# Running part of a layer norm under the attention of the layer before it

## The chip, the cores and the metric

The kernel runs on one core of one Trainium2 chip. The metric is the time of one execution on the device in microseconds (us), median of several runs; lower is better. Engines are named as in the profile: PE (TensorE matmuls), PEld (its weight loads), ACT (ScalarE), DVE (VectorE), POOL (GpSimd), SP (which issues DMAs). Each takes instructions from a queue of its own, in order, and waits on semaphores for the others.

## The reference

Four attention layers, alternately of kind A (segmented causal attention with a compressive memory) and B (full attention), work on x of shape 2048 x 512, each on a layer norm of x and added to x. There are 32 heads of 16 features.

```python
x = A_x
x = x + _A_ref(_layernorm(x), A_wq, A_wk, A_wv, A_wo, A_beta)   # layer 0
x = x + _B_ref(_layernorm(x), B_wqkv, B_wo)                     # layer 1
x = x + _A_ref(_layernorm(x), A_wq, A_wk, A_wv, A_wo, A_beta)   # layer 2
x = x + _B_ref(_layernorm(x), B_wqkv, B_wo)                     # layer 3
```

## The kernel before

The 2048 tokens are 16 tiles of 128. A layer has these stages: norm with transposes of all 16 tiles; projections; (A only) the memory; attention; output projection with residual. A small scheduler gathers operations in program order, tracks who reads and writes which buffer or PSUM bank, and puts in the semaphore waits. Each engine's queue has the order in which the operations were added. So the place of an `add` call in the program decides what stands behind what.

```python
def ln_stage1(self, t):                       # statistics, then the root on ACT
    sc.add("dve", ... e.bn_stats(st[:, 0:6], xt) ...)
    sc.add("dve", ... e.bn_aggr(st[:, 6:8], st[:, 0:6]) ...)
    sc.add("act", ... e.activation(st[:, 8:9], st[:, 7:8], ACT.Sqrt, bias=eps) ...)

def ln_stage2(self, t, evac_eng="act"):       # normalise, transpose, evict
    sc.add("dve", ... e.reciprocal(st[:, 9:10], st[:, 8:9]) ...)
    sc.add("dve", ... e.tensor_scalar(xn, xt, mean, rstd, op0=subtract, op1=mult) ...)
    bank = self.misc_bank()
    for c in range(NCH):                      # 4 transposes of 128x128 into one PSUM bank
        sc.add("pe", ... e.transpose(...) ...)
    sc.add("act", ... e.activation(xT tile t, bank, ACT.Copy) ...)

def ln_all(self, evac_eng="act"):
    LA = 2
    for t in range(min(LA, NT)):
        self.ln_stage1(t)
    for t in range(NT):
        if t + LA < NT:
            self.ln_stage1(t + LA)
        self.ln_stage2(t, evac_eng=evac_eng)
# [cut]
def layer_B(self, li):
    self.ln_all(...)
    ...                                       # K, Q and V projections; some are deferred
    self._misc_banks = [6, 7]
    for qc in range(4):                       # chunk of 512 queries
        for h in range(H):                    # a "pair": one head, one chunk
            for g in range(6):
                self.b_unit(...)              # 2 or 3 score matmuls (PE), one exp (ACT)
                if prev is not None and 1 <= g <= 4:
                    self.b_pv_part(*prev, g - 1, pstate)   # P.V of the pair before (PE)
                    ...                       # g == 4: its normalisation on DVE
                if g == 5 and work:
                    work.pop(0)()             # one outproj_T, outproj_mm or projection
    ...
    work.extend(outproj_items(3))             # the last four tiles: the "tail"
    self._misc_banks = list(range(8))
    while work:
        work.pop(0)()
# outproj_T(t):  4 transposes (PE), copy of the bank to xT (DVE)
# outproj_mm(t): 4 matmuls of 512 columns (PE), residual addition into x (DVE)
```

After the tail of one layer the next layer's norm starts. Six PSUM banks feed the exponentials, in two groups of three; the other two (6 and 7) take turns for P.V and all work that is slipped in at a pair's end.

The softmax here doesn't subtract the row's maximum and nothing guards it: scores larger than these inputs give would overflow.

## Time and profile before

| | |
|---|---|
| median of the first 4 runs | 2698.26 us (2697.51 to 2699.76) |
| span of the profiled run, mean granted PE clock | 2696.3 us, 0.965 |
| ACT, PE, DVE busy | 87%, 80%, 29% |
| last exponential of layer 1 to first projection matmul of layer 2 | 36.3 us |
| of this: last P.V and output projection of four tiles, then norm of layer 2 | 15 us, 21.5 us |

Times in a timeline are the start and the length of a group of equal instructions; the bracket gives the idle time of the engine before it and what ended that. First the page: busy times, and the costliest group (line, engine, operation, output and input, count; then busy us and mean ns; then idle us before and what ended most of it).

```profile
PE 2166.5 (80%) x26976; PEld 1242.6 (46%) x26976; DVE 778.4 (29%) x2571; ACT 2344.4 (87%) x2098; POOL 13.5 (1%) x19
...
L794 ACT ACTIVATE pT<-ps 128x1536 bf16<-128x1536 f32 (+1 forms) x1536 | 1877.9, 1317 | 112.8 <-PE ps L786 90.9
```

The exponentials of the two B layers (L794) are most of the time. The timeline of ACT at the start of layer 1's second chunk of queries shows how full ACT is. Six exponentials are one pair.

```profile
617.63 14.78 ACT L794 ACTIVATE pT<-ps 128x1536 bf16<-128x1536 f32 x12
632.90 14.78 ACT L794 ACTIVATE pT<-ps 128x1536 bf16<-128x1536 f32 x12 [0.48 <-PE ps L786]
648.16 14.78 ACT L794 ACTIVATE pT<-ps 128x1536 bf16<-128x1536 f32 x12 [0.49 <-PE ps L786]
663.43 14.78 ACT L794 ACTIVATE pT<-ps 128x1536 bf16<-128x1536 f32 x12 [0.49 <-PE ps L786]
```

In these pairs the output projection of the chunk before is slipped in, alternately four transposes and four matmuls. ACT has a gap only every second pair: after the matmuls. So PE can take four transposes per pair for nothing, and four 512-column matmuls cost ACT 0.49 us.

The timeline at the end of layer 1 (lines chosen) shows the stretch that the change is about. Its first line holds the last exponentials, which end at 1336.63.

```profile
1329.29 7.34 ACT L794 ACTIVATE pT<-ps 128x1536 bf16<-128x1536 f32 x6
...
1338.72 0.61 PE L843 MATMUL ps<-ident,tok 128*128 128x128 bf16 x4 [0.54 <-DVE tok L831]
1339.37 0.42 DVE L853 COPY xT<-ps 128x512 bf16<-128x512 bf16 x1 [0.70 <-PE ps L843]
1339.85 1.89 PE L864 MATMUL ps<-woB,xT 128*128 128x512 bf16 x4 [0.52 <-DVE xT L853]
1341.78 0.69 DVE L868 TENSOR_TENSOR x_tok<-x_tok,ps 128x512 bf16<-128x512 bf16 x1 [1.98 <-PE ps L864]
...
1344.78 0.69 DVE L868 TENSOR_TENSOR x_tok<-x_tok,ps 128x512 bf16<-128x512 bf16 x1 [1.98 <-PE ps L864]
...
1356.93 0.69 DVE L444 BATCH_NORM_STATS2 lnst<-x_tok 128x6 f32<-128x512 bf16 x1
1357.65 0.18 DVE L445 BATCH_NORM_AGGREGATE lnst<-lnst 128x2 f32<-128x6 f32 x1
1357.75 0.13 DVE L457 RECIPROCAL lnst<-lnst 128x1 f32<-128x1 f32 x1
1357.92 0.41 DVE L458 TENSOR_SCALAR xn_ring<-x_tok,lnst 128x512 bf16<-128x512 bf16 x1
1358.25 0.69 DVE L444 BATCH_NORM_STATS2 lnst<-x_tok 128x6 f32<-128x512 bf16 x1
...
1372.97 1.49 PE L495 MATMUL ps<-xT,wproj 128*128 128x512 bf16 x3
```

A tile's output projection takes 3.0 us (1341.78 to 1344.78). Its four matmuls take 1.89 us, 0.43 us each from issue to issue, against 0.22 us in mid-attention (there two score matmuls take 0.59 us and three 0.81 us). The clock granted to PE is 0.50 here (windows view, 1338 to 1350 us); the recorded texts call PE at this rate cold. The Trainium skill (TensorE: Matmul & The Clock Gate, "What's actually happening") describes a PE clock that halves after an idle window and rises again after a busy one; the factor of two agrees with this trace. In the norm, DVE has no idle time: 1.31 us a tile (1356.93 to 1358.25). ACT does the root and the eviction beside it, and has nothing else to do there.

### The profile page before, as it was taken

The page shows a single profiled execution, that of the slowest core. Times are in us where ns is not written, and L with a number is a line of the kernel's source. Part 1 is how long each engine was busy: PE and PEld are TensorE (multiplying, and loading weights), DVE is VectorE, ACT ScalarE, POOL GpSimd, SP SyncE. Part 2 cuts the span into 40 slices and gives each one's busy share as a digit, 9 for nine tenths or more (in the row PEclk, how much of TensorE's full clock was granted, in tenths as well). Part 3 has the DMA queues.
Part 4 walks back from the last instruction along what each step waited for, and adds up shares of the span by engine and source line. Part 5 has one row for each costly group of instructions (what it writes and reads, how often), then busy time and mean ns, then how long its engine had stood idle before and what let it go on. Part 6 is the DMA issues. An engine that isn't in the chain of part 4 may idle for free.

```text
span 2696.3 us, 62861 instructions
## 1 busy us (share of the span) xinstructions
PE 2166.5 (80%) x26976; PEld 1242.6 (46%) x26976; DVE 778.4 (29%) x2571; ACT 2344.4 (87%) x2098; POOL 13.5 (1%) x19
## 2 busy tenths in 40 slices
PE   6788788888888888888776887888888888888887
PEld 2465444444444444444434664444444444444444
DVE  6777732111111111111177776321111111111111
ACT  6488658999999999999863886689999999999997
POOL 1000000000000000000000000000000000000000
PEclk9799899999999999999977997999999999999998
DMA  2000000000000000000000000000000000000000
GB/s 71 24 2 2 1 1 2 25 2 2 1 2 2 1 2 2 2 2 2 1 1 24 2 2 2 1 1 2 2 1 9 2 2 9 2 1 2 9 2 9
DMA packets 9919, 15.56 MB, mean 6 GB/s; under 512 B 432, under 2 KB 8624, under 8 KB 9648
## 3 DMA queue, kind: packets, MB, share of 16 engines
q1 hardware_dynamic: 9648, 11.54, 1.3%
q8 instruction: 219, 3.59, 0.6%
q14 instruction: 52, 0.43, 0.1%
HBM read 9.45 MB, written 2.10 MB: 4 GB/s over the span
## 4 chain that ended last, share of the span: by engine, by line
ACT 51%; PE 30%; issue 14%; DVE 5%; DMA 0%; ACTq 0%; SPq 0%
ACT pT L794 45%; PE ps L786 11%; ACT pT L729 5%; PE ps L495 4%; PE ps L715 3%; PE ps L864 3%; PE ps L510 2%; PE ps L749 2%; PE ps L720 1%; PE ps L813 1%; PE ps L465 1%; DVE xn_ring L458 1%; DVE amem L664 1%; DVE lnst L444 1%; PE ps L843 1%
## 5 line engine op out<-in xcount | busy, mean ns | idle before, releaser
L794 ACT ACTIVATE pT<-ps 128x1536 bf16<-128x1536 f32 (+1 forms) x1536 | 1877.9, 1317 | 112.8 <-PE ps L786 90.9
L786 PE MATMUL ps<-qm,kT 128*128 128x512 bf16 x4096 | 1122.2, 377 | 369.5 <-ACT pT L794 274.2
L813 PEld LDWEIGHTS ps<-v_aug,pT 128*128 128x128 bf16 x16384 | 558.7, 96 | 244.5 <-ACT pT L794 1.7
L786 PEld LDWEIGHTS ps<-qm,kT 128*128 128x128 bf16 x4096 | 301.9, 96 | 769.8 <-PE ps L813 343.2
L813 PE MATMUL ps<-v_aug,pT 128*128 128x17 bf16 x16384 | 563.0, 171 | 1.5 <-ACT pT L794 1.5
L827 DVE RECIPROCAL small<-ps 128x4 f32<-128x4 f32 x256 | 46.9, 183 | 1499.7 <-PE ps L813 1499.7
L729 ACT ACTIVATE pT<-ps 128x1280 bf16<-128x1280 f32 x256 | 308.1, 1236 | 123.4 <-PE ps L720 119.5
L715 PE MATMUL ps<-qm,kT 128*128 128x512 bf16 (+3 forms) x1024 | 225.2, 301 | 5.4 <-DVE qm L686 4.8
L686 DVE TENSOR_SCALAR qm<-qT,blockmask_f 128x512 bf16<-128x512 bf16 x512 | 177.9, 349 | 88.4 <-PE ps L786 88.4
L720 PE MATMUL ps<-negmask,ident 128*128 128x128 bf16 x1024 | 184.1, 220 | 0.0
L749 PE MATMUL ps<-v_aug,pT 128*128 128x17 bf16 x2560 | 104.9, 172 | 38.9 <-ACT pT L729 36.3
L495 PE MATMUL ps<-xT,wproj 128*128 128x512 bf16 x512 | 126.4, 402 | 0.0
L715 PEld LDWEIGHTS ps<-qm,kT 128*128 128x128 bf16 x1024 | 99.8, 97 | 57.4 <-DVE qm L686 5.4
L749 PEld LDWEIGHTS ps<-v_aug,pT 128*128 128x128 bf16 x2560 | 82.3, 96 | 84.2 <-ACT pT L729 82.9
L720 PEld LDWEIGHTS ps<-negmask,ident 128*128 128x128 bf16 x1024 | 100.2, 98 | 2.8
L465 PE MATMUL ps<-ident,xn_ring 128*128 128x128 bf16 x256 | 38.2, 307 | 64.0 <-DVE xn_ring L458 64.0
L510 PE MATMUL ps<-wproj,xT 128*128 128x512 bf16 x384 | 84.7, 379 | 0.2 <-DVE phqT L543 0.2
L495 PEld LDWEIGHTS ps<-xT,wproj 128*128 128x128 bf16 x512 | 52.8, 103 | 66.9 <-issue 13.0
L768 DVE SCALAR_TENSOR_TENSOR tok<-tmpo,gcol,amem 128x64 bf16<-128x64 f32 x256 | 73.0, 285 | 9.1
L757 DVE RECIPROCAL small<-ps 128x4 f32<-128x4 f32 x256 | 46.8, 183 | 81.6 <-PE ps L749 71.6
L472 ACT ACTIVATE xT<-ps 128x512 bf16<-128x512 bf16 x64 | 37.6, 597 | 31.6 <-PE ps L465 31.6
L868 DVE TENSOR_TENSOR x_tok<-x_tok,ps 128x512 bf16<-128x512 bf16 x64 | 43.9, 685 | 63.5 <-PE ps L864 63.5
(60 smaller groups left out, 845.1 us busy)
## 6 DMA issues: line engine op xcount, KB each, us to landing
wproj<-in_B_wqkv_dram SPq DMA_DIRECT2D x2, 1536.0 KB, 6.4
x_tok<-in_A_x_dram SPq DMA_DIRECT2D x4, 512.0 KB, 5.4
out_dram<-x_tok SPq DMA_DIRECT2D x4, 512.0 KB, 2.9
wproj<-in_A_wq_dram SPq DMA_DIRECT2D x2, 512.0 KB, 5.8
wproj<-in_A_wk_dram SPq DMA_DIRECT2D x2, 512.0 KB, 6.9
wproj<-in_A_wv_dram SPq DMA_DIRECT2D x2, 512.0 KB, 7.5
woA<-in_A_wo_dram SPq DMA_DIRECT2D x1, 512.0 KB, 9.1
woB<-in_B_wo_dram SPq DMA_DIRECT2D x1, 512.0 KB, 9.2
```

Of the source, the lines that this page charges most:

```text
L495: sc.add("pe", (lambda lhsT, rhs, cin: lambda e: e.matmul(self.ps[:, bank.col0:bank.col0 + 512], lhsT, rhs, start=(cin == 0), stop=(cin == ...
L510: sc.add("pe", (lambda lhsT, rhs, cin: lambda e: e.matmul(self.ps[:, bank.col0:bank.col0 + 512], lhsT, rhs, start=(cin == 0), stop=(cin == ...
L686: sc.add("dve", lambda e: e.tensor_scalar(dst, src, mcol, None, op0=ALU.mult), reads=[self.b_qT[c][n + i] for i in range(4)] + [self.b_blo ...
L715: sc.add("pe", (lambda out_ap, lhsT, rhs: lambda e: e.matmul(out_ap, lhsT, rhs, start=True, stop=False))(out_ap, lhsT, rhs), reads=[kreads ...
L720: sc.add("pe", (lambda mask_out: lambda e: e.matmul(mask_out, self.ident[:], self.negmask[:], start=False, stop=True))(mask_out), reads=[s ...
L729: sc.add("act", lambda e: e.activation(dst, src, ACT.Exp, scale=float(SCALE)), writes=gr, bank_ops=[(B0, "r", alloc), (B1, "r", alloc), (B ...
L749: sc.add("pe", (lambda out_ap, lhsT, rhs, kb, qb: lambda e: e.matmul(out_ap, lhsT, rhs, start=(kb == 0), stop=(kb == qb)))(out_ap, lhsT, r ...
L768: sc.add("dve", lambda e: e.scalar_tensor_tensor(dst, tmpo, omg, am, op0=ALU.mult, op1=ALU.add), reads=[b_tmpo, self.b_gcol] + [self.b_ame ...
L786: sc.add("pe", (lambda out_ap, lhsT: lambda e: e.matmul(out_ap, lhsT, qmap, start=True, stop=True))(out_ap, lhsT), reads=[self.b_kT[c][kt] ...
L794: sc.add("act", lambda e: e.activation(dst, src, ACT.Exp, scale=float(SCALE)), writes=gr, bank_ops=[(banks[i], "r", alloc) for i in range( ...
L813: sc.add("pe", (lambda out_ap, lhsT, rhs, kt: lambda e: e.matmul(out_ap, lhsT, rhs, start=(kt == 0), stop=(kt == 15)))(out_ap, lhsT, rhs, kt),
L864: sc.add("pe", (lambda lhsT, rhs, c: lambda e: e.matmul(self.ps[:, bank2.col0:bank2.col0 + 512], lhsT, rhs, start=(c == 0), stop=(c == NCH ...
```

## The change

The layers become generators that yield after each step, and a driver lets the next layer advance by one step per pair of the present layer. A `need`/`done` table holds back what isn't ready. It does so only where the next layer is an A, so only between layers 1 and 2, and only for the norm: layer 2's projections still need the end of layer 1. Tiles 0 to 11 of x are final during layer 1 (after its chunks 0 to 2), tiles 12 to 15 only in its tail. So that ACT isn't burdened under the attention, the fused norm takes its root as a power of -0.5 on POOL and evicts on DVE. Core of the diff:

```diff
+    def ln_stage1(self, t, on_pool=False):
         ... bn_stats, bn_aggr ...
-        sc.add("act", ... ACT.Sqrt ...)
+        if not on_pool:
+            sc.add("act", ... ACT.Sqrt ...)
+            return
+        sc.add("dve", lambda e: e.tensor_scalar(st[:, 8:9], st[:, 7:8], float(LN_EPS), None, op0=ALU.add), ...)
+        sc.add("pool", lambda e: e.tensor_tensor(st[:, 9:10], st[:, 8:9], self.mhalf[:, 0:1], ALU.pow), ...)
 # [cut: ln_stage2 split into ln_stage2 (normalise) and ln_T (transpose, evict)]
+    def gen_A(self, li, fused_head):
+        for t in range(NT):
+            while s1 < NT and s1 <= t + LA:
+                if s1 > t and ("x", prev, s1) not in self.done:
+                    break
+                yield ("need", ("x", prev, s1))
+                self.ln_stage1(s1, on_pool=fused_head)
+                s1 += 1
+            self.ln_stage2(t, on_pool=fused_head)
+            if fused_head:
+                yield ("step", "norm")
+                if ("x", prev, 12) not in self.done:
+                    yield ("step", "norm")
+            self.ln_T(t, evac_eng=("dve" if fused_head else "act"))
+            yield ("step", "ln")
+        bank_fn = self.all_bank_rr()
+        yield ("need", ("end", prev))          # projections wait for the end of the layer before
 # [cut: the rest of gen_A and gen_B follows layer_A and layer_B, with ("done", ...) marks]
+    def drive(self):
+            fused = (li > 0) and self.fuse and kind == "A"
+        while cur < len(gens):
+            r = advance(cur)
+            ...
+            if self.fuse and nl < len(gens) and self.layers[nl] == "A" and cur in in_attn and nl not in in_attn:
+                for _ in range(self.fuse_steps):
+                    r2 = advance(nl)
```

## The prediction

> **What bounds the kernel.** The page gives ACT 87% busy of 2696.3 us, PE 80%, and a chain that ended last of which 45% is the B layers' exponentials. The timeline of ACT in the first B layer shows them back to back: 7.44 us per head-and-chunk pair. It also shows what extra PE work at a pair's end costs: four transposes alone, no ACT gap; four output-projection matmuls, a gap of 0.49 us; two projection groups, 1.35 us. So about 0.4 us of PE work per pair is free (4 x 0.215 us of matmul minus 0.49); the rest is lost.
>
> **What the change does.** Only a layer A that follows a layer B is fused, so of four layer norms one (layer 2's) moves: tiles 0 to 11 go under layer 1's attention, tiles 12 to 15 into its output-projection tail. The projections stay behind the end of layer 1. The reciprocal root moves from ACT (square root, 0.29 us, and table loads of 1.28 us) to a power on POOL; the eviction from ACT (0.60 us) to DVE (0.42 us by the outproj copies of the same shape).
>
> **What is on the path.** In the timeline around layer 1's end, the last exponential ends at 1336.6, four output projections take 3.0 us each to 1351.4, the norm runs at 1.31 us a tile (DVE-bound), and the first projection matmul of layer 2 starts at 1373.0. So about 21.5 us of norm is the most that can go. The table load before the norm falls in an ACT gap; the load back to exp falls where PE runs on through eight banks, so removing them gives almost nothing. The Trainium skill (ScalarE: Activation LUTs, What ACT_TABLE_LOAD costs) states about 1283 ns for the load; the trace agrees, 1283 ns.
>
> **What it costs back.** (1) The tail becomes serial. DVE runs its queue in order: tile t's residual, statistics, wait for the power, and normalisation stand ahead of tile t+1's outproj copy. From durations: residual 0.6, statistics 0.7, aggregate 0.2, add 0.15, power P, normalise 0.4, transposes, outproj matmuls at the cold clock 1.9: 4.7 us + P per tile against 3.0. The page shows no power on POOL; I estimate P at 0.6 us from its small operations (0.1 to 0.38). First residual at 1341.8, three periods, then 2.25 + P and 0.5 to the first projection matmul: 1358.5 + 4P, about 1361, against 1373.0: 12 us saved. (2) In attention, of each four transpose groups, one shares a boundary with outproj matmuls and one with outproj transposes; at the slack above that is about 0.4 us per chunk, 1.2 us over three chunks.
>
> Net about 10.5 us. **Predicted 2688 us, range 2683 to 2695.** Chances: faster by over 2% 0.01, within 2% 0.98, slower 0.01.
>
> **What would show it.** Right: from layer 1's last exponential to layer 2's first projection matmul shrinks from 36.4 to about 25 us, with tail tiles at 5 to 5.5 us each; new ACT gaps in layer 1 sum to 1 to 3 us; square roots on ACT fall from 64 to 48, table loads by two. Wrong: tail period still 3 us (then the saving nears 17), or the power over 1.5 us.
>
> **What would make it wrong.** A slow power on POOL: it enters the tail four times, and past 3 us the gain is gone; above 5 us DVE, waiting in order, would delay the P.V normalisations and so the two shared PSUM banks. Or the transposes breaking the ACT cadence for longer than one unit.

## The result, and the profile after

| | before | after |
|---|---|---|
| median | 2699.50 us (13 runs, 2697.51 to 2701.37) | 2688.05 us (9 runs, 2684.97 to 2689.26) |
| ratio | | 0.9956 (0.9946 to 0.9965) |
| ACT busy | 2344.4 us | 2329.7 us |
| last exponential of layer 1 to first projection matmul of layer 2 | 36.3 us | 23.9 us |

A ratio here is the mean time of one kernel's runs over that of the other's of the same rounds, so it is not quite the ratio of the medians. Executions over 1.5% slower than the fastest of the same kernel are left out of the means. The page's busy times and the same group of exponentials after:

```profile
PE 2164.2 (81%) x26976; PEld 1242.8 (46%) x26976; DVE 786.6 (29%) x2587; ACT 2329.7 (87%) x2064; POOL 22.6 (1%) x36
...
L859 ACT ACTIVATE pT<-ps 128x1536 bf16<-128x1536 f32 (+1 forms) x1536 | 1877.8, 1317 | 111.2 <-PE ps L851 89.3
```

ACT and its gaps at the same place in layer 1. The transposes of three of the chunk's four tiles of norm fall among them (649.5, 672 and 695 us); the fourth's, at 717 us, open no gap either:

```profile
635.13 14.78 ACT L859 ACTIVATE pT<-ps 128x1536 bf16<-128x1536 f32 x12 [0.49 <-PE ps L851]
650.62 14.78 ACT L859 ACTIVATE pT<-ps 128x1536 bf16<-128x1536 f32 x12 [0.71 <-PE ps L851]
665.88 14.74 ACT L859 ACTIVATE pT<-ps 128x1536 bf16<-128x1536 f32 x12 [0.48 <-PE ps L851]
681.11 19.02 ACT L859 ACTIVATE pT<-ps 128x1536 bf16<-128x1536 f32 x15 [0.49 <-PE ps L851]
```

One gap grew from 0.49 to 0.71 us, where transposes of the norm share a pair's end with output-projection matmuls. Three of the four groups cost nothing. From the first gap to the fourth takes 45.98 us (635.13 to 681.11) against 45.79 us before (632.90 to 678.69), and the same in the other two chunks: 0.6 us in all for twelve tiles of norm.

And the end of layer 1 (all engines, lines chosen; the last exponentials end at 1339.42):

```profile
1328.65 10.77 ACT L859 ACTIVATE pT<-ps 128x1536 bf16<-128x1536 f32 x9
...
1344.32 0.69 DVE L933 TENSOR_TENSOR x_tok<-x_tok,ps 128x512 bf16<-128x512 bf16 x1 [1.98 <-PE ps L929]
1345.04 0.69 DVE L455 BATCH_NORM_STATS2 lnst<-x_tok 128x6 f32<-128x512 bf16 x1
1345.77 0.18 DVE L456 BATCH_NORM_AGGREGATE lnst<-lnst 128x2 f32<-128x6 f32 x1
1345.98 0.15 DVE L461 TENSOR_SCALAR lnst<-lnst 128x1 f32<-128x1 f32 x1
1346.22 0.55 POOL L463 TENSOR_TENSOR lnst<-lnst,mhalf 128x1 f32<-128x1 f32 x1 [182.61 <-DVE lnst L461]
1346.80 0.41 DVE L476 TENSOR_SCALAR xn_ring<-x_tok,lnst 128x512 bf16<-128x512 bf16 x1 [0.66 <-POOL lnst L463]
1347.13 0.42 DVE L918 COPY xT<-ps 128x512 bf16<-128x512 bf16 x1
1347.27 0.61 PE L489 MATMUL ps<-ident,xn_ring 128*128 128x128 bf16 x4 [2.57 <-DVE xn_ring L476]
...
1347.67 1.91 PE L929 MATMUL ps<-woB,xT 128*128 128x512 bf16 x4
...
1349.62 0.69 DVE L933 TENSOR_TENSOR x_tok<-x_tok,ps 128x512 bf16<-128x512 bf16 x1 [1.28 <-PE ps L929]
...
1354.93 0.69 DVE L933 TENSOR_TENSOR x_tok<-x_tok,ps 128x512 bf16<-128x512 bf16 x1 [1.28 <-PE ps L929]
...
1359.29 0.69 DVE L933 TENSOR_TENSOR x_tok<-x_tok,ps 128x512 bf16<-128x512 bf16 x1 [0.55 <-PE ps L929]
...
1361.19 0.55 POOL L463 TENSOR_TENSOR lnst<-lnst,mhalf 128x1 f32<-128x1 f32 x1 [3.81 <-DVE lnst L461]
1361.69 0.55 POOL L645 MEMSET M_sb<- 128x544 f32 x1
1361.77 1.10 DVE L476 TENSOR_SCALAR xn_ring<-x_tok,lnst 128x512 bf16<-128x512 bf16 x1 [0.66 <-POOL lnst L463]
...
1363.33 8.40 PE L520 MATMUL ps<-xT,wproj 128*128 128x512 bf16 x32
```

From 1344.32 to 1349.62 this is one chain: tile 12's residual, statistics, power and normalisation, then two things side by side, tile 13's copy on DVE and tile 12's transposes on PE, and behind both tile 13's matmuls and its residual (1349.62). The transposes are the later of the two by a little: the matmuls start 0.12 us after the copy's end (1347.55 to 1347.67), against 0.06 us before (1339.79 to 1339.85). The period is 5.3 us against 3.0 before. For that, the pipelined norm of 16 tiles behind the tail is gone.

The two profiled spans differ by 9.1 us (2696.34 and 2687.26), and the sections add up to that. All are differences of starts or ends in the two traces:

| section | before | after | difference |
|---|---|---|---|
| start to layer 1's first exponential | 361.28 | 363.51 | +2.23 |
| to layer 1's last exponential (its end) | 975.34 | 975.91 | +0.56 |
| to layer 2's first projection matmul | 36.35 | 23.91 | -12.43 |
| to the end | 1323.37 | 1323.93 | +0.56 |

The first row can't be the change, as layer 0 has the same work in both (bar one small memset on POOL), and the first experiment below bears that out in its times. What differs there is the granted PE clock. This is the windows view of one stretch inside layer 0's attention (window, its length, then busy us of PE, PEld, DVE, ACT and POOL, then the granted PE clock), before:

```profile
212.00:225.00 13.00, 10.70 (x164) 7.46 (x162) 9.18 (x37) 9.96 (x9) 0.00 (x0) 1.00 0.00 1
```

and after:

```profile
212.00:225.00 13.00, 11.21 (x153) 7.54 (x152) 8.12 (x35) 10.21 (x9) 0.00 (x0) 0.87 0.01 1
```

The clock was 0.87 in this window in one run and 1.00 in the other. That accounts for 0.8 of the 2.23 us: exponentials of layer 0 start 1.41 us later than before up to this window (214.01 against 212.60) and 2.21 us later behind it (219.98 against 217.77). The first 1.41 us are there by 132 us already; what made them isn't shown here. Runs with a higher mean clock are the shorter ones: of the ten recorded runs of the changed kernel, the three with a mean clock of 0.969 took 2684.97 to 2685.23 us, the seven at 0.966 or 0.967 took 2686.89 to 2689.26 us. So a profile pair is good to some 3 us in its total, and sections have to be read one by one.

### The profile page after: what moved, and what is told of

The parts are those of the page before. It is cut to its first block, busy times and chain, and to the rows that moved or that the text cites. A ratio compares the mean times of both kernels' runs of the same rounds, so it can differ in the third digit from the quotient of the medians.

```text
span 2687.3 us, 62842 instructions
## 1 busy us (share of the span) xinstructions
PE 2164.2 (81%) x26976; PEld 1242.8 (46%) x26976; DVE 786.6 (29%) x2587; ACT 2329.7 (87%) x2064; POOL 22.6 (1%) x36
## 4 chain that ended last, share of the span: by engine, by line
ACT 51%; PE 30%; issue 14%; DVE 4%; DMA 0%; ACTq 0%; SPq 0%; POOL 0%; POOLq 0%
ACT pT L859 45%; PE ps L851 11%; ACT pT L794 5%; PE ps L520 4%; PE ps L780 3%; PE ps L535 3%; PE ps L929 3%; PE ps L814 2%; PE ps L785 1%; PE ps L878 1%; PE ps L489 1%; DVE amem L729 1%; DVE xn_ring L476 1%; PE ps L908 1%; DVE lnst L455 1%
## 5 line engine op out<-in xcount | busy, mean ns | idle before, releaser
L489 PE MATMUL ps<-ident,xn_ring 128*128 128x128 bf16 x256 | 35.5, 289 | 62.6 <-DVE xn_ring L476 62.6
L520 PEld LDWEIGHTS ps<-xT,wproj 128*128 128x128 bf16 x512 | 52.2, 102 | 65.5 <-issue 10.5
L896 DVE TENSOR_TENSOR tok<-ps,small 128x64 bf16<-128x64 f32 x256 | 57.5, 225 | 8.9
```

Of the source, the lines that this page charges most:

```text
L520: sc.add("pe", (lambda lhsT, rhs, cin: lambda e: e.matmul(self.ps[:, bank.col0:bank.col0 + 512], lhsT, rhs, start=(cin == 0), stop=(cin == ...
```

## The experiments

My theory: the gain is norm time taken off the path between the attentions of layers 1 and 2; twelve tiles run almost free under the attention, and the tail, now serial, gives part of it back. The rivals are named with each run. Each run is timed against the kernel before on the same chip, so ratios to before are compared, with 0.9956 for the change.

### 1. The new driver without fusing

```diff
-        self.fuse = True
+        self.fuse = False
```

> The changed kernel with fusing switched off: the new driver and generators, but every norm in its old place. My theory (the gain is layer 2's norm taken off the path): no gain, ratio to before 0.999 to 1.001. Rival (the restructured driver or another order of instructions elsewhere brings the gain): 0.996, as the changed kernel.

Measured: 2698.71 us against 2700.38 us, ratio 0.9998 (0.9985 to 1.001). The rewritten driver by itself changes nothing.

### 2. The new way of doing the norm, in the old place

```diff
-        self.fuse = True
+        self.fuse = False
 # gen_A
+        pool_head = li == 2
-                self.ln_stage1(s1, on_pool=fused_head)          # also ln_stage2, ln_T
+                self.ln_stage1(s1, on_pool=pool_head)
```

> Fusing off, but layer 2's norm done the new way where it always stood: power on POOL in place of ACT's square root (with its two table loads), eviction on DVE in place of ACT. Rival (ACT is the busiest engine, its busy time fell by 14.7 us from 2344.4 to 2329.7, and that relief is the gain of 11.5 us): about 2688 us, ratio 0.996. My theory (place matters, not relief; the norm is bound by DVE at 1.31 us a tile, and DVE now also takes the 0.42 us eviction and the 0.15 us addition while losing the 0.13 us reciprocal): slower than before by 16 x 0.35 to 0.45 us, plus up to 4 us of waits for the power, so 2703 to 2710 us, ratio 1.002 to 1.004.

Measured: 2716.00 us against 2700.38 us, ratio 1.0058 (1.0043 to 1.0074). The rival falls: ACT is relieved of the same work, and the kernel is 0.6% slower. But my size was too small as well: +15.6 us, not 3 to 10. The timeline of this kernel's norm shows why (lines chosen):

```profile
1360.24 0.41 DVE L476 TENSOR_SCALAR xn_ring<-x_tok,lnst 128x512 bf16<-128x512 bf16 x1
...
1360.71 0.61 PE L489 MATMUL ps<-ident,xn_ring 128*128 128x128 bf16 x4 [1.85 <-DVE xn_ring L476]
1361.35 0.42 DVE L499 COPY xT<-ps 128x512 bf16<-128x512 bf16 x1 [0.70 <-PE ps L489]
1361.69 0.68 DVE L455 BATCH_NORM_STATS2 lnst<-x_tok 128x6 f32<-128x512 bf16 x1
...
1362.70 0.40 DVE L476 TENSOR_SCALAR xn_ring<-x_tok,lnst 128x512 bf16<-128x512 bf16 x1
```

The period is 2.46 us a tile against 1.31, and the stretch between the two attentions takes 54.0 us in this trace against 36.3. I had added DVE's new work and some waits for the power. But the eviction stands in DVE's queue right behind the normalisation whose transposes it evicts, so DVE sits idle 0.70 us for PE, once per tile. On ACT that wait had cost nobody anything. Under the attention it is harmless again, as DVE is idle there most of the time (busy 81 of 705 us from 632 to 1337 us in the kernel before). So the moves to POOL and DVE are no gain of their own; they pay only where ACT is the bound.

### 3. Fused, with the eviction on ACT

```diff
-            self.ln_T(t, evac_eng=("dve" if fused_head else "act"))
+            self.ln_T(t, evac_eng="act")
```

> Fused as in the change, but the 16 evictions of layer 2's norm stay on ACT (0.60 us each). My theory (under the attention ACT is the bound, so each of the 12 evictions there costs its ACT time of about 0.5 us; the four in the tail are free): 6 us slower than the changed kernel, ratio to before about 0.998. Rival (ACT has slack there, because PE gaps of ACT already exist): under 2 us, ratio 0.996.

Measured: 2694.54 us, ratio 0.9977 (0.9963 to 0.999): 2.1 thousandths, 5.7 us, over the change's ratio. That is the 6 us expected, but the trace shows less. A chunk of 192 exponentials takes 240.8 us in it against 239.9 in the changed kernel, so the twelve evictions cost 2.7 us, 0.22 us each and not 0.5; in each chunk the first costs nothing, as it lies where ACT had the 0.71 us gap. The stretch behind is 0.36 us longer (24.27). The other 2.6 us are within the noise of the two ratios (0.0013 and 0.001 either way). So ACT has some free time there, and an eviction on ACT costs part of its length.

### 4. Fused, with the root on ACT

```diff
-                self.ln_stage1(s1, on_pool=fused_head)          # also ln_stage2
+                self.ln_stage1(s1, on_pool=False)
```

> Fused as in the change, but the root stays on ACT: each square root between exponentials brings a table load there and one back (1.28 us each by the trace) and 0.29 us of its own. My theory: 12 x 2.85 = 34 us at least under the attention[...]; plus 4 in the tail, of which some is hidden: slower than the changed kernel by 35 to 75 us, so 2720 to 2765 us, slower than before. Rival (the move to POOL was not needed, as table loads cost nothing here): 2688 us.

Measured: 2729.13 us, ratio 1.0105 (1.0091 to 1.0119): 41 us slower than the changed kernel and 1% slower than before. The groups of this kernel show the table loads (root, exponential of attention):

```profile
L458 ACT ACT_TABLE_LOAD x13 | 16.7, 1283 | 0.1
L859 ACT ACT_TABLE_LOAD x11 | 14.1, 1283 | 9.8 <-PE ps L851 9.8
```

In the changed kernel they are 3 and 2. The 19 extra loads are 24.4 us (a twentieth stands at L566, in layer 2's projections). Eighteen of them, 23.1 us, lie in layer 1's attention, which is 37.9 us longer than in the changed kernel (1013.80 against 975.90). The twelve roots there are 3.5 us more; the rest is waits behind them. Without the move to POOL the fusing would have lost.

### 5. Four extra powers per tile, in the tail only

```diff
+        if t >= 12:
+            for j in range(10, 14):
+                sc.add("pool", ... e.tensor_tensor(st[:, j:j + 1], st[:, 8:9], mhalf, ALU.pow) ...)
         sc.add("pool", lambda e: e.tensor_tensor(st[:, 9:10], st[:, 8:9], self.mhalf[:, 0:1], ALU.pow), ...)
```

> The changed kernel with four needless extra powers on POOL ahead of the real one, for tiles 12 to 15 only (the outproj tail). One power takes 0.55 us in the trace, so POOL's wait grows by 2.2 to 2.6 us per tile. My theory (in the tail the power is a link of the serial chain, once per tile): 4 x 2.2 to 2.6, 9 to 10.5 us slower than the changed kernel, about 2698 us, ratio to before 0.999 to 1.0. Rival (the tail is set by the cold output-projection matmuls, with the power hidden under them): 2688 us, ratio 0.996.

Measured: 2699.57 us, ratio 0.9991 (0.9975 to 1.0008): 3.5 thousandths, 9.5 us, over the change. The extra four take 2.43 us a tile in the trace, 9.7 us for four tiles. So the power is on the path once per tail tile, with its full length. The profiled run of this kernel fell into an odd state: 3191.99 us at a mean granted PE clock of 0.557 (0.56 in mid-attention too, 500 to 1500 us, where the changed kernel's trace has 1.00). I can't say why; it was the only such run, it is left out of the ratio, and only POOL durations are taken from its trace.

### 6. The same extra powers under the attention only

```diff
+        if t < 12:
```

> The same four extra powers, but for tiles 0 to 11 only (under the attention), so three times as many of them. My theory (DVE waits, but has nothing due for about 5 us after a pair's end): no cost, ratio 0.9945 to 0.9965 as the changed kernel. Rival (DVE's queue in order passes its wait on to the P.V normalisations and the shared banks): up to 12 x 2.4 = 29 us slower, ratio up to 1.006.

Measured: 2688.66 us, ratio 0.9951 (0.9936 to 0.9966). Three times as many extra powers as in run 5, no cost. DVE waited 29.7 us in all for POOL in this trace, and ACT's gaps are those of the changed kernel (0.49 and 0.71 us). Runs 5 and 6 are the same edit on and off the path.

### 7. The last four tiles' norm after the tail

```diff
         for t in range(NT):
+            if fused_head and t == 12:
+                yield ("need", ("end", prev))
```

> The changed kernel, but the norm of tiles 12 to 15 waits until all of layer 1's output projections are emitted, so nothing of it stands in the tail. My theory (interleaving in the tail gains nothing: 5.3 us a tile against 3.0 plus a pipelined norm at about 1.8 us a tile): last exponential to first projection matmul about 22 us against 23.9, so 0 to 3 us faster than the changed kernel, ratio 0.9945 to 0.996. Rival (interleaving hides the norm of the last four tiles under the output projection): 4 to 6 us slower, ratio 0.9975.

Measured: 2689.64 us, ratio 0.9957 (0.994 to 0.9974), no difference from the change; the stretch in the trace is 23.8 us (1338.50 to 1362.34) against 23.9, and not the 22 that I expected. So interleaving in the tail neither gains nor loses, and the rival that it hides these four tiles falls. What the change gains are the twelve tiles under the attention.

### 8. Fusing the B layers too

```diff
-            fused = (li > 0) and self.fuse and kind == "A"
+            fused = (li > 0) and self.fuse
-            if self.fuse and nl < len(gens) and self.layers[nl] == "A" and cur in in_attn and nl not in in_attn:
+            if self.fuse and nl < len(gens) and cur in in_attn and nl not in in_attn:
```

> The changed kernel with layers 1 and 3 (B, after A) fused too. Theory from the traces: each takes some 15 to 20 us of norm off the path, but layer A's attention has 1.49 us per pair with ACT waiting 0.26 us for PE in each, so PE has no slack and 12 transpose groups cost 0.25 to 0.4 us each (3 to 5 us a layer), and DVE, about 70% busy there, gets waits of 2 us per tile in front of the normalisations, which could cost up to 2 us a tile, 24 us a layer. So between 2660 and 2700 us; my point 2680, ratio 0.9925. Rival (slack for the norm exists in layer A's attention as in layer B's): 2688 less 2 x 11, 2666 us, ratio 0.9875.

Measured: 2700.46 us, ratio 0.9996 (0.9981 to 1.0011). The whole gain of the change is lost; the time lies at the pessimistic end of my expectation (2700), far from its point (2680). In layer 0 the attention grew by 19.5 us (first exponential to the end of the last: 127.83 to 328.54 us, against 127.04 to 308.30 us in the changed kernel), while the stretch to layer 1's first exponential shrank by 13.2 us (55.2 to 42.0): +6.2 us. In layer 2 the attention grew by 19.8 us and the stretch to layer 3's first exponential shrank by 16.9 us: +2.8 us. These 9.1 us are most of the 11.9 us between the two profiled spans; of the rest, 1.8 us lie in layer 3's attention and 0.8 us ahead of layer 0's first exponential, places that this run didn't change. The waits of 165 to 300 us (who waited for whom: us, times, longest) in the changed kernel:

```profile
ACT pT L794 <- PE ps L785: 20.8, 41, 2.0
```

and with the B layers fused:

```profile
ACT pT L794 <- PE ps L785: 36.2, 51, 1.6
...
PE ps L489 <- DVE tmpo L828: 7.5, 9, 0.8
```

A pair of layer A's attention takes 1.3 to 1.5 us where one of layer B takes 7.44 us, and DVE is busy 101.6 of these 135 us (99.9 in the changed kernel). The norm's transposes (L489) wait for a PSUM bank that DVE has yet to read, and ACT waits for PE behind them. So fusing the B layers doesn't pay here, and the change leaves them out.

### 9. The serial tail broken up in the B layers

```diff
-        work.extend(outproj_items(3))
+        tail = outproj_items(3)            # all four transposes and copies first, copies on ACT
+        work.extend(tail[0::4] + tail[1::4] + [it for i in range(4) for it in (tail[4 * i + 2], tail[4 * i + 3])])
 # gen_A, after ln_stage1
+            if fused_head and t >= 12:
+                if t > 12:
+                    self.ln_stage2(t - 1, on_pool=True)
+                    self.ln_T(t - 1, evac_eng="act")
+                if t == NT - 1:
+                    self.ln_stage2(t, on_pool=True)
+                    self.ln_T(t, evac_eng="act")
+                yield ("step", "ln")
+                continue
```

> The changed kernel with the serial tail broken up, in both B layers: the four transpose groups of the last outproj tiles go first, their copies on ACT (idle there); then the four output-projection groups; in layer 2's norm a tile's normalisation and transposes are queued only after the next tile's statistics, with the eviction on ACT. My theory (the 5.3 us per tile of the changed kernel is one chain residual, statistics, power, normalisation, next copy, next matmuls): the period falls to DVE's own work of about 2.0 to 2.3 us a tile, so last exponential to first projection matmul about 16 us against 23.9, 7 to 8 us less, and 2 us less at layer 3's end: 2676 to 2680 us, ratio about 0.9915. Rival (the tail is bound by the cold PE): 2686 us, ratio 0.995.

Measured: 2677.23 us, ratio 0.9917 (0.9902 to 0.9932). The time is as expected, but its parts aren't: the stretch is 19.0 us (1338.56 to 1357.59), not 16, 4.9 us less than the changed kernel's, and layer 3's end, from its last exponential to the end of the profile, is 6.0 us shorter (12.15 against 18.17), not 2. The timeline of this kernel (lines chosen) has the reason:

```profile
1349.38 0.69 DVE L933 TENSOR_TENSOR x_tok<-x_tok,ps 128x512 bf16<-128x512 bf16 x1 [1.87 <-PE ps L929]
...
1351.12 0.40 DVE L476 TENSOR_SCALAR xn_ring<-x_tok,lnst 128x512 bf16<-128x512 bf16 x1
...
1351.58 0.61 PE L489 MATMUL ps<-ident,xn_ring 128*128 128x128 bf16 x4 [2.24 <-DVE xn_ring L476]
1351.98 1.91 PE L929 MATMUL ps<-woB,xT 128*128 128x512 bf16 x4
...
1353.94 0.69 DVE L933 TENSOR_TENSOR x_tok<-x_tok,ps 128x512 bf16<-128x512 bf16 x1 [2.41 <-PE ps L929]
```

I had cut the chain in DVE's queue only. In PE's queue a tile's transposes still stood ahead of the next matmuls, so DVE and PE waited for each other in turn, with a period of 4.56 us. The two sections make up 10.9 of the 11.2 us between the two profiled spans. How much of the 6.0 us is the order and how much the granted clock (mean 0.972 against 0.966), no run here separates.

### 10. The A layers' tails in the new order too

```diff
+        self._misc_banks = list(range(8))
         for i in range(4):
             t = 4 * (NSEG - 1) + i
             self.outproj_T(t, evac_eng="act")
             yield ("done", ("tok2free", li, t))
+        for i in range(4):
+            t = 4 * (NSEG - 1) + i
             self.outproj_mm(t, self.woA, self.b_woA)
```

> The run before, with the A layers' four last outproj tiles in the same order too (all transposes and copies first, then the matmuls, with all eight banks). In the trace those tiles take 3.0 us each; the matmul groups alone take 1.9 us at the cold clock. My theory: about 2 us less for each of two A layers, 2672 to 2676 us, ratio about 0.990. Rival (the tile period of 3.0 us is set by the matmuls alone): no difference to the run before.

Measured: 2667.01 us, ratio 0.9882 (0.9865 to 0.9898), 10 us less than run 9 where I expected 4. In the traces the stretch from an A layer's last exponential to the B layer's first is 5.6 us shorter than in run 9 after layer 0 (49.7 against 55.3) and 5.7 us after layer 2 (49.6 against 55.3). In layer 0 the matmuls of all four tiles took 3.63 us together in the trace, not 1.9 us each: PE went from one group to the next with the full clock. From the last exponential to the first statistics it took 6.7 us, against 11.2 us in the changed kernel.

### 11. The chain cut in PE's queue as well

```diff
             if fused_head and t >= 12:
-                if t > 12: ...                       # as in run 9
+                if t == NT - 1:
+                    for tt in range(12, NT):
+                        self.ln_stage2(tt, on_pool=True)
+                        self.ln_T(tt, evac_eng="act")
                 yield ("step", "ln")
                 continue
```

> The run before (outproj tails in the new order in all layers), but in layer 2's norm all four tail tiles get their statistics and powers first, and normalisation and transposes stand behind the last output-projection matmul in PE's queue. In the ninth and tenth runs a tile's transposes stood ahead of the matmuls of the tile after next, and the tail kept a period of 4.5 us for its last two tiles. My theory: with that link gone DVE sets the tail (residual, statistics, aggregate, addition: 1.75 us a tile, then four normalisations of 0.45), so last exponential to first projection matmul about 15 us, against 19 to 20; 4 to 5 us less than the run before: 2661 to 2664 us, ratio about 0.9865. Rival (PE's matmuls at the cold clock, 1.9 us a group, set it): no less than the run before.

Measured: 2661.23 us, ratio 0.9853 (0.9836 to 0.9869). The stretch is 15.2 us (1334.55 to 1349.73), as expected, with a period of 1.74 us for residual and statistics on DVE, while the 16 matmuls ran in one go. This is the best version: 1.5% below before, over three times the gain of the change. All of the extra came from the order of instructions and from copies moved to an idle engine. No run has this order without the fusing, so how much of it the fusing is needed for stays open.

### 12. The memsets away from the last normalisation

```diff
-        sc.add("pool", lambda e: e.memset(self.M_sb[:], 0.0), writes=self.b_M, name="M0")
+        sc.add("pool", lambda e: e.memset(self.M_sb[:], 0.0), reads=[self.b_v[3]], writes=self.b_M, name="M0")
```

> The changed kernel, but POOL's two memsets of layer 2's memory wait for a v tile of that layer, so they no longer run right behind the last power. In the changed kernel's trace the last normalisation on DVE took 1.10 us against 0.41 us for the others, and lay beside these memsets. If the memsets hold DVE up: that normalisation takes 0.41 us and the stretch from last exponential to first projection matmul falls by 0.7 us to about 23.2 us. If it was long for another reason: still about 1.1 us and 23.9 us. The time itself moves by less than its scatter either way.

Measured (one look): correct, 2689.28 us. The last normalisation:

```profile
1362.15 0.41 DVE L476 TENSOR_SCALAR xn_ring<-x_tok,lnst 128x512 bf16<-128x512 bf16 x1 [0.66 <-POOL lnst L463]
```

It takes 0.41 us in place of 1.10, and the stretch is 23.2 us (1339.79 to 1363.02) in place of 23.9. So POOL's memsets held DVE up. That agrees with the Trainium skill (SBUF — State Buffer, "SBUF: two separate sides"): DVE and GpSimd share a pair of ports under an exclusive lock, held for a whole instruction, against a DVE instruction that is in a two-port mode. Which mode the normalisation is in, no run here shows. In the changed kernel the two memsets run from 1361.69 to 1362.73 us, and DVE's 1.10 us end right behind them, at 1362.87.

## Why the prediction was right

The time, 2688.05 us, lies on the point (2688), inside the range, and within 2%. That it meets the point so closely is luck: the runs scatter by 4 us, P was a guess from other small operations, and by the traces the two sized terms give 11.9 us (12.4 less 0.6), not 10.5. The steps held as well:

- **What is on the path.** The stretch between the two attentions shrank by 12.4 us; 12 were predicted. Runs 1 and 2 exclude the driver and ACT's relief as causes; runs 5, 6 and 7 place the gain in the twelve tiles under the attention.
- **The serial tail.** Predicted 4.7 us + P with P = 0.6, so 5.3 us; measured 5.30 and 5.31 us for two tiles. The power took 0.55 us. Run 5 shows that it enters once per tail tile. Two small things that I hadn't foreseen nearly cancel: the last tail tile took 4.4 us, because its matmuls ran at the full clock (granted 1.00 from 1356 to 1359 us; 1.04 us in place of 1.9), and the last normalisation was held up 0.7 us by POOL's memsets (run 12).
- **The cost under the attention.** Predicted 0.4 us per chunk, 1.2 us in all; measured 0.19 and 0.6 us. This term was mis-sized by a factor of two: transposes beside output-projection matmuls cost 0.22 us (the gap of 0.71), but transposes beside transposes, for which I had put in a cost, cost nothing. The new gaps do not reach the 1 to 3 us that the prediction named as its sign. That ACT's time is dear there is shown by run 4, and by run 3 at less than half the size expected.
- **Counts.** Roots on ACT fell from 64 to 48 and table loads from 9 to 7, as predicted. What removing those loads is worth by itself no run isolates; run 2 removes them as well, and is slower.
- **Layer 3 doesn't shift quite rigidly:** from layer 2's first projection matmul to the end the profiles differ by 0.56 us. The traces point to the granted clock. Counted from that matmul, layer 3's first exponential comes 2.3 us later in the changed kernel, and in the 60 us ahead of it the clock is 0.69 against 0.77; over the next 10 us it is 1.00 against 0.83, and 1.7 of the 2.3 us are won back. That nothing else differs there isn't shown.

## What to carry to other kernels

Cost a piece of work by the place in which it runs: the same norm costs 1.31 us a tile between two attentions, 0.05 us a tile under layer B's attention, and more than it saves under layer A's (run 8). Work moved under a busy stage is best taken off that stage's bound engine (the roots left on ACT cost 41 us in run 4, the evictions 2.7 us by the trace of run 3), and here the move to another engine paid only there (run 2). Where several engines share a tail, write down the order of every queue and look for the chain that runs back and forth between them; cutting it in one queue alone leaves the other (run 9), and cutting it in both, with the tails of all layers reordered (run 11), was worth more here than the change itself.

## What the Trainium skill lacked or had wrong

- ScalarE: Activation LUTs, "Rules for kernel authors", calls ScalarE the only option for a square root. Here POOL takes a reciprocal root as a power of -0.5, 128x1 in 0.55 us, with a correct result and without a table load; GPSIMD Engine Reference doesn't list the power or its time.
- ScalarE: Activation LUTs, "What ACT_TABLE_LOAD costs", puts a drain of about 1380 ns beside the load's 1283 ns. The load is confirmed (1283 ns in every kernel here). In run 4 no separate drain shows: of one pair, the exponentials end at 662.6 us, the load starts at 662.61, and the root at 663.90.
- SBUF — State Buffer, "SBUF: two separate sides", gives the lock between DVE and GpSimd, but no case of two memsets on POOL holding a normalisation up; here 1.10 us in place of 0.41 (run 12).
- TensorE: Matmul & The Clock Gate explains cold and warm matmuls; no page gives the scatter of a whole kernel's time that goes with the granted clock: here 2685 us at a mean clock of 0.969 and 2687 to 2689 us at 0.966 or 0.967 for the same kernel. The run at 0.557 and 3192 us is explained by no page that I know of.
